# Seven block products for eight in the last two pairs of units, gate, value and output projection

## The chip, the cores and the metric

One core of one Trainium2 chip runs the program. The metric is device time in microseconds for one execution; the time before is the median of three runs.

## The reference

Chunk-selecting causal attention, then a gated feed-forward layer. For q, k, v of shape 4 x 8 heads x 768 x 64, keys stand in 24 chunks of 32; each query keeps the six chunks with the largest upper bound of its scores.

```python
ub = sum_d max(q * k_min[chunk], q * k_max[chunk])      # causal chunks only
top_chunks = argsort(ub)[..., -6:]
scores = where(selected & causal, q @ k.T / 8, -1e9)
x = softmax(scores) @ v                                  # laid out as 3072 tokens x 512
out = (sigmoid(x @ w_gate) * (x @ w_val)) @ w_out        # w_gate, w_val: 512 x 1536; w_out: 1536 x 512
```

The output is 3072 x 512 in float32.

## The kernel before

The 3072 tokens are taken in eight units u0 to u7 of 384 (three row tiles of 128). A unit first chooses chunks (`prepare`), then attends (`attend`: score products `sc`, exponentials `exp` on ACT, the causal mask `cm` on POOL, value products `pv`, and `finish`, which normalises on DVE with `rz` and `x` and turns x by a DMA transpose `xT` on SP for units u4 to u7), and then goes through the feed-forward layer. x of a unit lies as `xT`, four tiles of 128 channels by 384 tokens, in fp16; the three weight matrices stay in SBUF in fp16 (`wg16`, `wv16`, `wo16`).

Plain units (`ffn`, lines 898 to 927) make, for each of 12 blocks of 128 hidden columns, four gate matmuls and four value matmuls of 384 columns (line 913), `tanh` on ACT (line 921) and `hg = (tanh + 1) * value` on DVE (line 925), whose value operand is the product itself in PSUM. `project_out` (lines 929 to 957) then makes, for each of three row tiles, 12 matmuls of 512 columns (line 944; three instructions o0, o1, o2 of four), evicts on ACT or DVE with a factor 0.5 (`osb`, lines 953 and 954) and stores 256 KB through SP (`out`).

One pair of units, u5 with u6, goes through `ffn_pair` (line 977). Two units side by side, two halves of the channels and two halves of the hidden columns make 2 x 2 blocks, and seven products of blocks stand for eight. Four sums T of x blocks (line 993, DVE) and four sums each of gate and value weights (Sg, Sv in `mixed`, line 972, DVE) are formed first. For each of six pairs of hidden blocks, gate and value each need products P1 to P7 of two matmuls of 384 columns (line 1022), which collect in three PSUM banks. Three of the four results pass through SBUF: E (an eviction by ACT or DVE) and C (a sum on DVE, line 1037); the fourth stays in PSUM. `tanh` (line 1047) and `hg` (line 1052) follow, and for three of the four results `hg` reads its value from SBUF. Output projection of the pair is `project_out`, as for the others.

Nothing is ordered at run time. A string ORDER lists every instruction group in one sequence, with the engine where there is a choice (`@POOL`) and the numbers of the buffers it takes; each engine runs its share of the list in that order, and waits come from the data and from the reuse of buffers. There are eight PSUM banks (products named u, q, r, o, g, v share them), seven `np` buffers for the C sums, 18 `hg` buffers, six `v`, two `big`, two `qf` and one `qm`.

Of the kernel before, what the change touches and what calls it, by code (L numbers as in the profile page):

```python
# [162 lines left out]
sc_u3_7_2:2 v_3_1:5 rz_u3_1:0 x_u3_1:1 tanh_u2_7 sc_u3_4_0:5 exp_u3_4_0 cm_u3_4 hg_u2_7 exp_u3_7_2 exp_u3_4_2 hg_u2_6
sc_u3_7_1:0 exp_u3_7_1 g_u2_8:3,0,12 tanh_u2_8 v_u2_8:5 g_u2_9:7,1,13 sc_u3_4_1:3 v_u2_9:0 v_2_0:1 pv_u3_5:2
hq0_u4_0@POOL ubn0_u4:0 ubn1_u4 ubm0_u4 mx0_u4:0 ubm1_u4 hk0_2_3@DVE out_u1_2 tanh_u2_9 mx1_u4 hk0_2_2@DVE v_2_4:3
ap0_u4 apt0_u4:0 hk0_2_0@ACT hg_u2_8 g_u2_10:7,3,14 exp_u3_4_1 tanh_u2_10 v_u2_10:6 hg_u2_10 hg_u2_9 xps_u3_1:3,1
cm_u3_7 hq1_u4_2@POOL pv_u3_7:7 hq1_u4_0@POOL g_u2_11:1,2,15 v_u2_11:5 v_2_5:2 tanh_u2_11 hg_u2_11 o0_u2_0:6,1 o1_u2_0
xT_u3_1 hqm0_u4_0 sc_u4_1_3:3,0 exp_u4_1_3 hqm0_u4_2@DVE xps_u3_0:5 k11_3 qf0_u6_0:1 xT_u3_0 sc_u4_0_0:0,1 exp_u4_0_0
sc_u4_0_3:1 qf0_u5_1 qm_u5_0@ACT:0 pv_u3_4 rz_u3_2:0 x_u3_2:2 pv_u3_6 rz_u3_3:1 ap1_u4 x_u3_3:1 sc_u4_1_1:5 qf0_u6_3
k10_3 k16_3_3@DVE:6 sc_u4_1_2:0 exp_u4_1_2 qf0_u6_2 qf0_u5_2 qf0_u6_1 o2_u2_0 sc_u4_3_3:2,2 exp_u4_3_3 exp_u4_1_1  # L170
sc_u4_2_3:3,3 exp_u4_2_3 v_3_4:4 o0_u2_1:4,0 qm_u5_2 sc_u4_1_0:2 exp_u4_1_0 apt1_u4 sc_u4_0_2:5 exp_u4_0_2 o1_u2_1
v_1_5:0 sc_u4_2_1:2 exp_u4_2_1 kx0_3_1 kx1_3_3:1 kx0_3_0 hq1_u5_0@POOL sc_u4_2_0:5 v16_2_0 v16_2_4 v16_1_5 o2_u2_1
cm_u4_1 osb_u2_1 out_u2_1 sc_u4_0_1:2 exp_u4_0_1 exp_u4_0_3 k16_3_0:0 exp_u4_2_0 q10_3:1 osb_u2_0 out_u2_0 q00_3
sc_u4_3_1:3 exp_u4_3_1 ub_u5:7,0 ubn0_u5:0 hqm1_u4_0 pv_u4_1:5 sc_u4_5_0:6,0 cm_u4_0 pv_u4_0 rz_u4_0:1 sc_u4_4_0:3,1
xps_u3_2:7 xps_u3_3:1 hq0_u5_0@ACT o0_u2_2:2,0 sc_u4_5_1:4 o1_u2_2 hq1_u5_2@POOL exp_u4_5_0 exp_u4_4_0 xT_u3_3
hqm1_u4_2@DVE x_u4_0:1 o2_u2_2 xT_u3_2@ACT hk1_2_3@ACT exp_u4_5_1 g_u3_0:7,2,0 tanh_u3_0 sc_u4_5_2:4 exp_u4_5_2
sc_u4_5_3:5 sc_u4_4_3:3 exp_u4_4_3 v_u3_0:6 g_u3_1:7,1,12 tanh_u3_1 sc_u4_4_2:3 exp_u4_4_2 exp_u4_5_3 sc_u4_4_1:4
exp_u4_4_1 v_u3_1:1 g_u3_2:7,3,13 tanh_u3_2 ubn1_u5 v_u3_2:5 g_u3_3:4,0,14 hg_u3_0 tanh_u3_3 cm_u4_4 pv_u4_4:7 hk1_2_2
sc_u4_6_3:3,1 osb_u2_2 hq0_u5_2@POOL kx1_3_2 sc_u4_6_1:6 exp_u4_6_1 v_u3_3:0 sc_u4_3_0:2 exp_u4_3_0 v_3_0:0 v_2_3:3
v16_2_3 kx1_3_1 hg_u3_1 mx0_u5:0 hg_u3_2 sc_u4_6_0:4 cm_u4_5 pv_u4_5 g_u3_4:6,3,15 sc_u4_7_2:2,0 sc_u4_6_2:5 tanh_u3_4  # L180
cm_u4_2 exp_u4_6_2 hg_u3_3 exp_u4_6_3 v_u3_4:0 g_u3_5:6,0,2 tanh_u3_5 sc_u4_2_2:3 ap0_u5 sc_u4_7_0:5 exp_u4_7_0
exp_u4_6_0 cm_u4_6 v_u3_5:1 q01_3 g_u3_6:6,1,16 tanh_u3_6 v_u3_6:4 g_u3_7:6,2,17 tanh_u3_7 v_u3_7:5 apt0_u5:0
hqm0_u5_0 mx1_u5 q11_3 qf1_u6_1 qf1_u6_3 hg_u3_4 qf1_u6_2 ap1_u5 hg_u3_5 rz_u4_2:1 x_u4_2:2 xT_u4_2:0 hg_u3_6
qf0_u7_0:0 v_3_2:3 g_u3_8:4,1,1 tanh_u3_8 apt1_u5 qf1_u6_0 v16_2_5 v_u3_8:6 g_u3_9:7,0,3 sc_u4_3_2:4 tanh_u3_9 hg_u3_7
exp_u4_3_2 kx0_3_3 sc_u4_7_1:5 exp_u4_7_1 exp_u4_2_2 v_u3_9:1 exp_u4_7_2 sc_u4_7_3:7 exp_u4_7_3 hqm1_u5_2@DVE hg_u3_8
hqm0_u5_2@DVE g_u3_10:6,1,4 tanh_u3_10 cm_u4_3 pv_u4_6:5 v_3_3:1 pv_u4_3:3 hg_u3_9 sc_u5_0_2:1,1 exp_u5_0_2
sc_u5_0_0:2 sc_u5_1_1:7,2 sc_u5_0_1:6 exp_u5_0_1 exp_u5_0_0 pv_u4_2 rz_u4_1:1 x_u4_1:2 v_u3_10:1 hg_u3_10
qm_u6_2@ACT:0 hq1_u6_2@POOL cm_u4_7 pv_u4_7 hq0_u6_2 kx0_3_2 v_2_2:2 out_u2_2 g_u3_11:3,0,5 tanh_u3_11 sc_u5_3_0:1,0
sc_u5_7_1:2,3 v_u3_11:6 exp_u5_1_1 k16_3_1@ACT:5 v16_3_1 sc_u5_1_0:3 exp_u5_1_0 hq0_u6_0@POOL exp_u5_3_0 sc_u5_7_0:7
# [85 lines left out]
def pe(busy, lag=170):  # L275
    return {PE: (busy, busy + lag)}
# [3 lines left out]
def kernel(  # L280
# [10 lines left out]
    nc = tc.nc  # L291
# [667 lines left out]
    def mixed(w16, name, key, prio, raw):  # L959
# [10 lines left out]
        for i, x, op, y, need in ((0, a21, ALU.add, a22, []), (1, s(0), ALU.subtract, a11, [(t, 0)]),  # L970
# [3 lines left out]
            op.deps += [(o, False) for o in users]  # L974
        return t

    def ffn_pair(ua, ub_, base, span):

        next_ = rank(base, span, 6 * 32 + 2 * 15)
        EV = 0.1  # L980
# [225 lines left out]
```

## Time and profile before

| | |
|---|---|
| median of three runs | 290.27 us (290.11 to 291.36) |
| the profiled execution's own time | 289.61 us |
| its span in the profile | 287.9 us |
| busy: PE, DVE, ACT, POOL | 271.2, 222.2, 192.5, 115.3 us |
| granted TensorE clock | 1.00 |

The profile is of one execution. Busy time of an engine is the time in which at least one of its instructions ran; matmuls overlap one another, so the duration of one is longer than what it adds to the stream. The profiled execution's own time is larger than its span, since it holds what lies around the instructions, and it is one run beside the three of the median.

### The profile page before, as it was taken

Reading aid. Unit: us, or ns where it says so; the run is one execution under the profiler, and the core shown is the slowest. Engines: PE = TensorE matmul, PEld = TensorE weight load, DVE = VectorE, ACT = ScalarE, POOL = GpSimd, SP = SyncE. Lnnn points to the kernel's source line nnn. Section 1 sums busy time; section 2 is a strip of 40 time slices with the busy share of each in tenths; the row PEclk is TensorE's granted clock in tenths of the full one; section 3 lists DMA queues with packets and bytes.
Section 4 is the critical chain, followed back from the end, with each engine's and each line's share of the span. In section 5 each row is a group of like instructions: output and inputs, shape, how many; then the busy total and the mean of one; then the engine's idle time right before and its main releaser. Section 6 shows DMA issues by size and latency. Waiting matters only on the chain.

```text
span 287.9 us, 6927 instructions
## 1 busy us (share of the span) xinstructions
PE 271.2 (94%) x2596; PEld 173.0 (60%) x2596; DVE 222.2 (77%) x607; ACT 192.5 (67%) x403; POOL 115.3 (40%) x181
## 2 busy tenths in 40 slices
PE   1858999899999999999999999999999999999995
PEld 0636565667765666666767556578656666555543
DVE  7568987589998999996796999796899988831121
ACT  2477489697788876678759656578879996432320
POOL 7297735246166835656234874462131002000000
PEclk9999999999999999999999999999999999999999
DMA  7999999999999947969906221002300000101112
GB/s 162 242 231 221 214 196 201 211 176 218 184 192 193 207 88 134 215 130 184 182 20 149 59 68 50 2 14 67 88 28 2 15 16 12 56 36 73 53 59 109
DMA packets 130033, 34.26 MB, mean 119 GB/s; under 512 B 118096, under 2 KB 127056, under 8 KB 130000
## 3 DMA queue, kind: packets, MB, share of 16 engines
q1 hardware_dynamic: 125248, 29.11, 47.7%
q0 software_dynamic: 4752, 4.72, 9.8%
q8 instruction: 20, 0.33, 0.5%
q14 instruction: 13, 0.11, 0.1%
HBM read 30.67 MB, written 6.29 MB: 128 GB/s over the span
## 4 chain that ended last, share of the span: by engine, by line
PE 64%; DVE 13%; DMA 11%; ACT 4%; SPq 3%; issue 3%; POOL 1%; DVEq 0%; POOLq 0%; ACTq 0%
PE o_u L944 16%; PE v_u L913 11%; PE g_u L913 10%; PE sc_u L824 9%; PE pv_u L857 5%; DMA kq_u<-in_q_dram 4%; DMA v<-in_v_dram 3%; PE sug_u5u L1022 3%; PE suv_u5u L1022 3%; ACT att_u L835 2%; DVE hg_u L925 2%; SPq L503 2%; DMA q<-in_q_dram 2%; PE ube_u L763 2%; PE srv_u5u L1022 1%
## 5 line engine op out<-in xcount | busy, mean ns | idle before, releaser
L835 ACT ACTIVATE att_u<-sc_u 128x512 f16<-128x512 f32 (+3 forms) x184 | 90.8, 548 | 20.6 <-PE sc_u L824 19.4
L841 POOL TENSOR_SCALAR_AFFINE_SELECT att_u<-att_u 128x384 f16<-128x384 f16 (+1 forms) x56 | 30.0, 546 | 81.6 <-ACT att_u L835 71.4
L944 PE MATMUL o_u<-wo,hg_u 128*128 128x512 f16 (+1 forms) x252 | 59.5, 376 | 0.0
L913 PE MATMUL v_u<-xT_u,wv 128*128 128x384 f16 x288 | 58.6, 326 | 0.2 <-ACT gate_u L921 0.2
L913 PE MATMUL g_u<-xT_u,wg 128*128 128x384 f16 x288 | 58.6, 326 | 0.0
L925 DVE SCALAR_TENSOR_TENSOR hg_u<-gate_u,v_u 128x384 f16<-128x384 f16 x72 | 38.1, 541 | 25.0 <-PE v_u L913 16.3
L921 ACT ACTIVATE gate_u<-g_u 128x384 f16<-128x384 f32 x72 | 35.0, 494 | 24.0 <-PE g_u L913 23.5
L944 PEld LDWEIGHTS <-hg_u 128*128 128x128 f16 x264 | 24.5, 98 | 23.6 <-issue 0.7
L913 PEld LDWEIGHTS <-wv 128*128 128x128 f16 x288 | 27.5, 98 | 17.1 <-issue 1.4
L913 PEld LDWEIGHTS <-wg 128*128 128x128 f16 x288 | 27.2, 98 | 16.7 <-issue 0.5
L824 PE MATMUL sc_u<-hqo,hko 128*128 128x128 f16 (+2 forms) x220 | 27.9, 243 | 0.4 <-DVE osb_u L954 0.4
L857 PEld LDWEIGHTS <-att_u 128*128 128x128 f16 x640 | 24.6, 97 | 5.8 <-issue 1.9
L824 PE MATMUL sc_u<-hqe,hke 128*128 128x128 f16 (+2 forms) x220 | 27.8, 243 | 0.2 <-ACT att_u L835 0.2
L857 PE MATMUL pv_u<-v,att_u 128*128 128x65 f16 x640 | 26.9, 193 | 0.8 <-POOL v L540 0.7
L953 ACT ACTIVATE osb_u<-o_u 128x512 f32<-128x512 f32 (+1 forms) x17 | 10.1, 592 | 18.2 <-PE o_u L944 13.6
L824 PEld LDWEIGHTS <-hke 128*128 128x128 f16 x220 | 17.2, 98 | 7.5 <-issue 0.4
L824 PEld LDWEIGHTS <-hko 128*128 128x128 f16 x220 | 16.8, 98 | 6.0 <-issue 0.7
L540 POOL CAST v<-v 128x512 f16<-128x512 f32 x23 | 14.2, 620 | 9.4 <-DMA v<-in_v_dram 6.9
L876 DVE TENSOR_TENSOR x_u<-pv_u,rz_u 128x384 f16<-128x384 f32 (+1 forms) x28 | 14.8, 531 | 0.5
L786 DVE MAX8 mx_u<-ubn_u 128x8 f32<-128x8 f32 (+16 forms) x152 | 12.5, 156 | 0.1
L730 DVE STREAM_TRANSPOSE qf_u<-q 128x384 f32<-128x384 f32 (+2 forms) x28 | 11.8, 440 | 0.4 <-DMA q<-in_q_dram 0.3
L548 DVE TRANSPOSE_TENSOR_REDUCE kx<-k 128x24 f32<-128x768 f32 x12 | 11.2, 952 | 0.2 <-DMA k<-in_k_dram 0.2
(179 smaller groups left out, 450.5 us busy)
## 6 DMA issues: line engine op xcount, KB each, us to landing
v<-in_v_dram SPq DMA_DIRECT2D x23, 256.0 KB, 5.0
out_dram<-osb_u SPq DMA_DIRECT2D x23, 256.0 KB, 2.3
k<-in_k_dram SPq DMA_DIRECT2D x12, 384.0 KB, 5.5
q<-in_q_dram SPq DMA_DIRECT2D x12, 384.0 KB, 5.5
wg<-in_moe_w_gate_dram POOLq DMA_DIRECT2D x3, 512.0 KB, 10.3
wv<-in_moe_w_val_dram POOLq DMA_DIRECT2D x3, 512.0 KB, 11.5
wo<-in_moe_w_out_dram POOLq DMA_DIRECT2D x3, 512.0 KB, 19.0
qf<-in_q_dram SPq DMA_DIRECT2D x8, 128.0 KB, 3.3
```

The lines of the kernel that those rows point to most:

```text
L540: plan.add(f"v16_{b}_{ib}", {POOL: pool(H * D)}, lambda e: nc.gpsimd.tensor_copy(v16[b % 2][:, ib, :, 0:D], at(t)), reads=[t], writes=[("v ...
L786: nc.vector.max(at(mx)[:, e_, j, :], at(ubn)[:, e_, j, 0:max(8, u.seen[j])])
L824: nc.tensor.matmul(at(t)[:, o:o + 128 * m], hk[b % 2][e_][:, p, 128 * jb:128 * jb + 128], hq[u.side][e_][:, p, 128 * x:128 * (x + m)], sta ...
L835: plan.add(f"exp_{u.name}_{h}_{y}", {ACT: act(n)}, lambda e, t=t, att=att, b0=b0, n=n: nc.scalar.activation(at(att)[:, b0:b0 + n], at(t), ...
L841: nc.gpsimd.affine_select(out=dv, in_=dv, compare_op=ALU.is_ge, fill=0.0, base=0, pattern=[[0, u.m], [1, 128]], channel_multiplier=-1)
L857: nc.tensor.matmul(at(pv)[:, last, x, :], at(att)[:, c:c + 128], v16[b % 2][:, jb, h, :], start=(jb == 0), stop=(jb == ib))
L876: plan.add(f"x_{u.name}_{p}", {DVE: dve(u.t)}, lambda e: nc.vector.tensor_tensor(at(x_).rearrange("p a (e d) -> p e a d", e=2), at(pv)[:, ...
L913: nc.tensor.matmul(at(t), w16[:, c, 128 * fb:128 * fb + 128], at(u.xt)[:, c, :], start=(c == 0), stop=(c == 3))
L921: plan.add(f"tanh_{u.name}_{fb}", {ACT: act(T)}, lambda e, g=g, gate=gate: nc.scalar.activation(at(gate), at(g), AF.Tanh, scale=0.5), read ...
L925: plan.add(f"hg_{u.name}_{fb}", {DVE: dve(T)}, lambda e, w_=w_, gate=gate, hg=hg: nc.vector.scalar_tensor_tensor(at(hg), at(gate), 1.0, at ...
L944: nc.tensor.matmul(at(o), hgs[c][1][1]()[:, 128 * tb:128 * tb + 128], wo16[:, fc, lo:hi], start=(c == 0), stop=(c == NFB - 1))
L1022: nc.tensor.matmul(at(t), left[i](c), right[i](c), start=first and c == 0, stop=c == 1, skip_group_check=not first)
```

## The change

- Pairs are now u4 with u5 and u6 with u7; u6 is no longer paired with u5, and no unit after u3 goes through `ffn` or `project_out`.
- `ffn_pair` gets two parameters: where T lies (`qm` for the first pair, `qf` for the second) and whether the pair is the last one, whose `hg` of the second unit lies in `att` buffers. x of u6 and u7 share one buffer of eight tiles (`x0` is a unit's first tile in it).
- The output projection of a pair is also made of seven block products, in `project_pair`. Blocks are the two units, the two halves of the hidden columns and the two halves of the 512 output columns. For each of six pairs of hidden blocks four sums S1 to S4 of `hg` tiles (128 x 384, fp16, all operands in SBUF) are formed on DVE or POOL; S3 overwrites one of its inputs, the others go to buffers that attention has left (`v16`, `hq`, `hk`). Four sums So of w_out blocks are formed once on DVE (`mixed_out`).
- For each of three row tiles of a pair, products Q1 to Q7 of six matmuls of 256 columns collect in three PSUM banks. Each of the four output quarters starts with F (ACT or DVE, factor 0.5; one is F alone) and is completed by G (DVE, PSUM times 0.5 plus the quarter in SBUF). Q6, Q7 and Q4 add to a bank that F or G has read in between. The last tile of u7 is stored in two halves of 256 columns, all others as 512.
- ORDER is new from the point where u2's attention has ended and u3's has begun, ahead of u2's feed-forward layer, with other choices of engine for copies and evictions. Up to there it is the same.

```diff
+    def mixed_out():
...
+        b11, b12, b21, b22 = (wo16[:, a:a + half, n:n + 256] for a in (0, half) for n in (0, 256))
...
+        for i, x, y in ((0, b12, b11), (1, b22, t[0]), (2, b22, b12), (3, b21, t[1])):
+            op = plan.add(f"So{i}", {DVE: dve(D_FF, 1.8)}, lambda e, i=i, x=x, y=y: nc.vector.tensor_tensor(t[i], x, y, ALU.subtract),
...
+    def project_pair(ua, ub_, hg, homes, next_):
...
+        for f in range(half):
...
+            a11, a12, a21, a22 = hg[0, f], hg[0, f + half], hg[1, f], hg[1, f + half]
+            sums[3, f] = a21
+            for i, x, op_, y in ((1, a21, ALU.add, a22), (2, sums[1, f], ALU.subtract, a11), (3, a11, ALU.subtract, a21), (4, a12, ALU.subtract, sums[2, f])):
+                o = sums[i, f]
+                op = plan.add(f"S{i}_{tag}_{f}", {DVE: dve(T, 2), POOL: (960, 1000)}, lambda e, o=o, x=x, op_=op_, y=y: (
+                    nc.vector if e == DVE else nc.gpsimd).tensor_tensor(o[1](), x[1](), y[1](), op_),
...
+        what = {1: (11, lambda f: wo16[:, f, 0:256]), 2: (12, lambda f: wo16[:, f + half, 0:256]), 3: (4, lambda f: wo16[:, f + half, 256:512]),
+                4: (22, lambda f: so[3][:, f]), 5: (1, lambda f: so[0][:, f]), 6: (2, lambda f: so[1][:, f]), 7: (3, lambda f: so[2][:, f])}
...
+        for tb in range(3):
+            u_, q_, r_ = (ps(f"{c}o_{tag}_{tb}", c, [128, 256]) for c in ("su", "sq", "sr"))
...
+                    for f in range(half):
+                        nc.tensor.matmul(at(t), sums[what[i][0], f][1]()[:, 128 * tb:128 * tb + 128], what[i][1](f),
+                                         start=first and f == 0, stop=f == half - 1, skip_group_check=not first)
...
+            op = mul(1, u_, True)
...
+            keep_(0, u_, ka, oa, 0)
+            mul(2, q_, True)
+            add(0, q_, ka, oa, 0)
+            mul(5, r_, True)
+            keep_(3, r_, kb, ob, 256)
+            mul(6, u_, False)
+            keep_(1, u_, ka, oa, 256)
+            mul(3, r_, False)
+            add(1, r_, ka, oa, 256)
+            store(0, ka, oa, 0, 512)
+            mul(7, u_, False)
+            add(3, u_, kb, ob, 256)
+            mul(4, u_, False)
+            keep_(2, u_, kb, ob, 0)
+            if ub_ is units[7] and tb == 2:
+                store(1, kb, ob, 256, 512)
+                store(1, kb, ob, 0, 256)
+            else:
+                store(1, kb, ob, 0, 512)
...
-    ffn(units[4], 5.0, 0.95)
...
-    ffn_pair(units[5], units[6], 6.4, 1.6)
+    so = mixed_out()
+    ffn_pair(units[4], units[5], 6.0, 1.9, "qm", False)
...
-    ffn(units[7], 8.0, 0.95)
+    ffn_pair(units[6], units[7], 8.0, 1.9, "qf", True)
```

In ORDER, `mul`, `keep_` and `add` of `project_pair` are the entries Q, F and G.

More of the change, by code (lines that the diff above doesn't have):

```diff
@@ L163 @@
[L163 to L177, printed above, removed]
@@ L975, in mixed, with ffn_pair @@
         return t
-    def ffn_pair(ua, ub_, base, span):
+    def ffn_pair(ua, ub_, base, span, home, last):
         next_ = rank(base, span, 6 * 32 + 2 * 15)
@@ L996, in ffn_pair @@
         hgb = [Buf("v", f"hgp_{ub_.name}_{f}", [128, 2, T], F16) for f in range(half)]
+        if last:
+            hgb = [Buf("att", f"hgp_{ub_.name}_{f}", [128, 2, 2, T], F16) for f in range(0, half, 2) for _ in range(2)]
+            hgb = [hgb[f // 2 * 2] for f in range(half)]
         hg = {}
@@ L1078, in ffn_pair @@
                 plan.hold(first_, b)
-        for x, u in ((0, ua), (1, ub_)):
-            project_out(u, [(fb, hg[x, fb]) for f in range(half) for fb in (f, f + half)], [], next_)
+        if last:
+            out_home = Buf("big", f"osb_{tag}", [128, 3, 2, 512])
+            homes = {(tb, x): ((out_home, tb, x), lambda tb=tb, x=x: at(out_home)[:, tb, x]) for tb in range(3) for x in range(2)}
+        else:
+            home_ = Buf("qm", f"osb_{tag}", [128, 2, 512])
+            homes = {(1, x): ((home_, x), lambda x=x: at(home_)[:, x]) for x in range(2)}
+            for tb in (0, 2):
+                for x, u in ((0, ua), (1, ub_)):
+                    b = Buf("osb", f"osb_{u.name}_{tb}", [128, 512])
+                    homes[tb, x] = ((b, 0), lambda b=b: at(b))
@@ new lines, in ffn_pair, with held @@
+        project_pair(ua, ub_, hg, homes, next_)
+    def held(keys):
+        found = {}
+        for key in keys:
+            if key in plan.writer:
+                found[plan.writer[key]] = False
+            for o in plan.readers.get(key, ()):
+                found[o] = False
+        return list(found.items())
+    def mixed_out():
+        views = [hk[0][e].rearrange("p a s -> p (a s)").rearrange("p (i f n) -> p i f n", i=2, n=256) for e in range(2)]
+        half = NFB // 2
+        b11, b12, b21, b22 = (wo16[:, a:a + half, n:n + 256] for a in (0, half) for n in (0, 256))
+        t = [views[i // 2][:, i % 2] for i in range(4)]
+        free = held([("hk", 0, jb, e, p) for jb in range(NBLK) for e in range(2) for p in range(NP)] +
+                    [("hkp", 0, e, p) for e in range(2) for p in range(NP)])
+        for i, x, y in ((0, b12, b11), (1, b22, t[0]), (2, b22, b12), (3, b21, t[1])):
+            op = plan.add(f"So{i}", {DVE: dve(D_FF, 1.8)}, lambda e, i=i, x=x, y=y: nc.vector.tensor_tensor(t[i], x, y, ALU.subtract),
+                          reads=[("wo", j) for j in range(3)] + ([("So", i // 2)] if i % 2 else []), writes=[("So", i)], port=True, prio=6.9 + 0.02 * i)
+            op.deps += [d for d in free if d not in op.deps]
+        return t
@@ L1082 @@
     for u in units:
-        u.xt = Buf("qf" if u.i >= 7 else "xt", f"xT_{u.name}", [128, 4, T], F16)
+        u.xt, u.x0 = Buf("xt", f"xT_{u.name}", [128, 4, T], F16), 0
+    units[6].xt = units[7].xt = Buf("qf", "xT_u6u7", [128, 8, T], F16)
+    units[7].x0 = 4
     raw_f = {b: load_first(b, -10.0 + b) for b in range(3)}
```

284 lines of the change are left out of this document (189 added, 95 removed).

## Prediction

> **What bounds the kernel now.** I read the page's engine shares first, then the waits of PE after its start-up, then busy time by windows, and last the chain of waits with the tables by form, for what one instruction costs.
>
> ```profile
> PE 271.2 (94%) x2596; PEld 173.0 (60%) x2596; DVE 222.2 (77%) x607; ACT 192.5 (67%) x403; POOL 115.3 (40%) x181
> ```
>
> ```profile
> PE ube_u L763 <- DVE hg_u L925: 0.4, 1, 0.4
> PE sc_u L824 <- DVE osb_u L954: 0.4, 1, 0.4
> PE v_u L913 <- ACT gate_u L921: 0.2, 1, 0.2
> ```
>
> ```profile
> 0.00:20.00 20.00, 9.98 (x67) 7.54 (x67) 11.85 (x23) 8.42 (x13) 12.31 (x26) 1.00 0.94 210
> 20.00:40.00 20.00, 18.73 (x155) 12.62 (x156) 18.64 (x72) 12.98 (x29) 12.97 (x20) 1.00 1.20 214
> 40.00:60.00 20.00, 18.97 (x191) 12.00 (x190) 12.83 (x44) 16.54 (x44) 8.77 (x19) 1.00 1.03 194
> ...
> 212.00:252.00 40.00, 40.00 (x360) 25.62 (x358) 36.75 (x78) 31.83 (x72) 2.98 (x6) 1.00 0.07 18
> ...
> 280.00:288.00 8.00, 4.67 (x34) 2.65 (x32) 0.98 (x2) 0.63 (x2) 0.00 (x0) 1.00 0.26 98
> ```
>
> The three waits are all that PE has from 60 us to the end: 1.0 us in sum. The windows' columns are PE, weight load, DVE, ACT and POOL busy, then the granted clock, the DMA share and GB/s. Of 16.7 us in which PE is idle (287.9 less 271.2), 12.3 lie before 60 us, in start-up, and 3.3 behind the last matmul. In between, PE is the bound: a microsecond of matmul taken out there shortens the run by one, unless another engine takes the place. DVE is the next candidate: in the stage where the one existing block-product pair runs (212 to 252 us) it is busy 36.75 of 40 us with 78 instructions, yet PE waited for nothing. POOL worked only 2.98 us there. That row is the yardstick below.
>
> **PE: what goes and what comes.**
>
> ```profile
> 231.43 0.65 PE suv_u5u L1022 x4
> ...
> 241.30 0.91 PE pv_u L857 x30
> ...
> 248.49 0.65 PE g_u L913 x4
> ...
> 258.71 5.18 PE o_u L944 x24
> ```
>
> ```profile
> L944 PE MATMUL o_u<-wo,hg_u 128*128 128x512 f16 x240 | 57.6, 379 | 0.0
> ...
> L824 PE MATMUL sc_u<-hqo,hko 128*128 128x256 f16 x44 | 9.4, 273 | 0.0
> ```
>
> In the chain, four matmuls of 384 columns take 0.65 us (0.1625 each, plain or block product alike), and 24 of 512 take 5.18 (0.216 each). The durations by form include a latency that overlaps the next matmul: 379 ns for 512 columns against 216 of advance. With 256 columns fewer the duration is 106 ns shorter (273), so such a matmul advances PE by about 0.109 us. Weight loads keep up: the page has 173.0 us for 2596 of them, 67 ns each. Gone: the plain gate and value of units u4 and u7, 2 x 96 matmuls x 0.1625 = 31.2 us; the plain projection of u4 to u7, 4 x 36 x 0.216 = 31.1 us (one tile is split in two, same columns). New: one more gate/value pair, 6 x 2 x 7 products x 2 matmuls = 168 x 0.1625 = 27.3 us; two projections, 2 x 3 row tiles x 7 products x 6 matmuls = 252 x 0.109 = 27.5 us. Net **-7.5 us**. The other pair exists already and only changes partners. These are upper values of what the products save; nothing else leaves PE.
>
> **DVE, ACT, POOL: what the products cost elsewhere.** The second pair adds 36 evictions E (ACT or DVE), 36 sums C (DVE) and four T. The projections add 48 sums S (35 on POOL, 13 on DVE), four So and, for six evictions of 512 columns per pair, 12 F and 9 G of 256. The new order moves copies off DVE: 58 instead of 73. I weigh this where it must fit tightest: the last stage, from T0 of u6/u7 to its first projection product Q1.
>
> ```profile
> 222.21 0.54 DVE L1037 TENSOR_TENSOR c3g_u5u<-c3g_u5u,sug_u5u 128x384 f32<-128x384 f32 x1
> 222.67 0.54 DVE L1037 TENSOR_TENSOR c1g_u5u<-c1g_u5u,srg_u5u 128x384 f32<-128x384 f32 x1
> ```
>
> ```profile
> L635 DVE TENSOR_TENSOR xf<-pvf,rzf 128x256 f16<-128x256 f32 x8 | 3.3, 418 | 0.1
> ...
> L972 DVE TENSOR_TENSOR Sg<-wg 128x1536 f16<-128x1536 f16 x2 | 1.8, 912 | 0.0
> ...
> L555 POOL TENSOR_TENSOR kcr<-kx,kcr 128x96 f32<-128x96 f32 x2 | 0.8, 388 | 0.1
> ...
> L555 POOL TENSOR_TENSOR kcr<-kx_u,kcr 128x48 f32<-128x48 f32 x1 | 0.3, 276 | 0.0
> ```
>
> Sums start 0.46 us apart though each shows 0.54; so DVE's own advance is 0.08 below the duration. The written order puts into that stage, on PE, 84 gate/value products x 0.325, 21 products of the u4/u5 projection x 0.655 and two attention products of 15 matmuls each (30 take 0.91 in the chain): 42.0 us. On DVE: 34 C and 24 hg x 0.465 = 27.0; 11 G and F of 256 columns x 0.33 = 3.6; two So x 0.87 = 1.7; four T x 0.46 = 1.8; seven S, taken as 0.27 (half a T of twice the width; at most 0.46) = 1.9; two for the last normalisation, at most 0.9. Together 84 instructions, 36.9 us. That is 2.0 per us of PE, where the yardstick has 1.95 and PE does not wait. ACT has no exponentials left there and is under 30 us. So by load alone PE keeps its lead, with about 5 us of room.
>
> What the yardstick lacks is POOL. Two points of POOL's tensor-tensor (276 ns at 48 columns, 388 at 96) give 2.33 ns a column, so an S of 384 takes about 1.06 us, an estimate along that line; 21 of them and one mask are 23 us in the 42, against 2.98 in 40 now.
>
> ```profile
> 208.63 1.31 POOL L841 TENSOR_SCALAR_AFFINE_SELECT att_u<-att_u 128x384 f16<-128x384 f16 x2 [5.65 <-ACT att_u L835]
> 210.00 1.03 POOL L333 COPY hqo<-apt_u 64x768 f16<-64x768 f16 x1
> ```
>
> ```profile
> 206.22 0.55 DVE L993 TENSOR_TENSOR T_u5u<-xT_u,xT_u 128x768 f16<-128x768 f16 x1
> ...
> 210.27 1.17 DVE L993 TENSOR_TENSOR T_u5u<-xT_u 128x768 f16<-128x768 f16 x1
> ```
>
> ```profile
> L1052 DVE SCALAR_TENSOR_TENSOR hgp_u<-gate_u5u,c1v_u5u x6: 551/552/679, 220.7 to 250.4; 128x384 f16<-128x384 f16 x6
> ```
>
> A T takes 0.55 us with POOL idle, and 1.17 when begun inside POOL's copy (210.00 to 211.03): it ends about 0.4 us after that copy, as if it had stood still until then. One hg, whose gate and sum both lie in SBUF, took 679 ns instead of 552. The page "SBUF — State Buffer" of the Trainium skill, section "Who interferes with whom", says that a DVE instruction with two SBUF inputs and a GpSimd instruction that reads SBUF exclude each other for a whole instruction, the later one waiting; this trace agrees for the T (1.17 against 0.55), and the rule speaks against putting S on POOL beside hg.
>
> In the last stage 31 DVE instructions read two SBUF tensors: 18 of the 24 hg (the other six take PSUM), seven S, two So, four T. C, G and F read PSUM. If POOL is inside an instruction for 23 of 42 us and a collision costs half an S (0.53 us), 31 x 0.55 x 0.53 = 9 us would be added to DVE's 36.9, 3.9 more than PE's 42.0. Bounds: no collisions, zero; every one of the 31 meeting a running S, 16.4 us added, 11.3 over. I take **+2.5 us**, nearer the middle estimate than zero, since POOL's S come in bursts and a queued S must then wait for DVE in turn. In the u4/u5 pair before it, attention of u6 and u7 lies between, so PE has more to do per DVE instruction; I put stalls there at zero. If that cover fails, the price is again some 0.5 us per collision.
>
> **The end, and the queues.**
>
> ```profile
> out_dram<-osb_u SPq DMA_DIRECT2D x23, 256.0 KB, 2.3
> ```
>
> The row 280 to 288 has PE busy for its first 4.67 us: its last matmul ends at 284.67, and eviction and last store take the 3.2 us to 287.9. After the change the last eviction has 256 columns and its store half of this row's 256 KB: no loss, and a gain that I leave at zero. But six row tiles of u6 and u7 leave together: 1.5 MB in about the last 5 us, where the row 280 to 288 shows 98 GB/s at a DMA share of 0.26, that is 377 GB/s at full use or 4.2 us for them. They nearly fit; I add **0.3 us** (0 to 0.7). On SP the stores queue only behind one another. What may stall at the seam is T1 and T3 of u6/u7, which wait for the transpose by DMA of u7's last head pair and hold the DVE instructions ordered behind them (G, F and S of u4/u5). Ahead of the first product that needs them PE has nine projection products and two gate products, 6.5 us, against about 1 for normalising and a transfer like the stores' 2.3: hidden, and if not, some 1 us.
>
> Two dependencies are new on PE: the weights' differences So stand on DVE well ahead of the products that read them, so nothing; and products 6, 7 and 4 add into the bank that F and G have just read, so each waits for that read. In the order two or three products (1.3 to 2.0 us) of other row tiles lie between, once only one (0.65 us), for a read of about 0.4: zero, at most 0.3.
>
> **The sum.** Against the profiled execution: span 287.9 - 7.5 + 2.5 + 0.3 = 283.2 us; its own time is 289.61, 1.7 above its span, and the median of the runs, 290.27, lies 0.66 higher still. Carried over, 290.27 - 4.7 = **285.6 us**.
>
> **Rivals.**
> - No contention that counts: POOL's S fall beside C, G and F, which do not meet it. For: six of ten DVE instructions in the stage are of that kind, and POOL has 19 us to wait in. Against: the 1.17 us row. 290.27 - 7.5 + 0.3 = 283.1 us. Chance 0.22.
> - DVE and POOL become the bound of the last stage, slower than before. Place: from T0 of u6/u7 to Q1; price per collision 0.53 us. It decides from the point where the waits exceed the 5.1 us of room by the 7.2 that are left of the gain: 12.3 us, 0.40 us on each of the 31. With every one of them meeting an S: 290.27 - 7.5 + 0.3 + 11.3 = 294.4 us. For: all S of a unit pair wait for the hg that run at the same time. Against: POOL has work for only 55% of the stage. By the Trainium skill's rule (same page and section), taken strictly, the middle estimate of 3.9 would stand instead of 2.5, and the sum would be 287.0. Chance 0.16.
> - The new order leaves holes of its own, for instance at the seam or in the redrawn middle part, where half of the 7.5 us vanish from PE while DVE gets more to do. One hole as long as the seam's whole cover, 6.5 us, eats the gain: 290.27 - 7.5 + 0.3 + 6.5 = 289.6 us. Chance 0.10.
> - That the change does not do what it says is excluded by the listing of instructions: 588 pair and projection matmuls of u4 to u7 stand where 516 of larger size stood.
>
> **How the numbers follow.** The forecast, 284 to 288 us, has 0.52. A measurement of this kernel can tell about 0.5% (1.5 us) from no change. Faster by more than that (below 288.8): forecast 0.52, no contention 0.22 and a tenth of the third rival, 0.75. Within it: 0.09, the rest of the third rival. Slower: 0.16. The range goes from 282.0 (no contention, and the whole 1.0 us of PE's present waits gone) to 291.5, which takes in the third rival and the weak end of the second.
>
> **What would show it.** In the profile after: PE with about 36 matmuls of 512 columns for each of u0 to u3 only, and 252 of 256 columns at an advance of 0.11; PE busy about 264 us. POOL's S near 1.06 us each. In the last 55 us, hg with both inputs in SBUF at a mean clearly above 552 ns, C unchanged at 550, and PE's waits of 2 to 4 us naming hg, E or S. Wrong it would be if PE waits before that stage, if hg keeps 552 ns beside a busy POOL, or if PE's waits name POOL's S alone.

## The result and the profile after

| | before | after |
|---|---|---|
| median of four runs each, side by side | 290.19 us | 285.88 us |
| ratio, 95% interval | | 0.986 [0.982, 0.990] |
| the profiled execution, span | 287.9 us | 284.5 us |
| busy PE, DVE, ACT, POOL | 271.2, 222.2, 192.5, 115.3 us | 265.6, 248.8, 209.5, 162.1 us |

The forecast was 285.6 us. A second comparison, of six runs with 17 of before, gave 0.988 [0.983, 0.993].

The page's engine shares of after, and then the waits of PE from 60 us to the end (engine, tile and line, what it waited for; us in total, times, longest):

```profile
PE 265.6 (93%) x2668; PEld 180.9 (64%) x2668; DVE 248.8 (87%) x660; ACT 209.5 (74%) x457; POOL 162.1 (57%) x231
```

```profile
PE sqg_u4u L1054 <- DVE x_u L900: 0.7, 1, 0.7
PE srg_u6u L1054 <- DVE hg_u L1084: 0.5, 1, 0.5
PE sug_u4u L1054 <- DVE c3g_u4u L1069: 0.3, 1, 0.3
...
```

All rows of that view together hold 1.9 us, against 1.0 before. Busy time by windows of after (PE, weight load, DVE, ACT, POOL, granted clock, DMA share, GB/s):

```profile
200.00:220.00 20.00, 19.14 (x186) 12.53 (x185) 19.46 (x39) 18.63 (x43) 13.57 (x17) 1.00 0.08 17
220.00:240.00 20.00, 19.48 (x198) 15.01 (x196) 18.56 (x42) 12.22 (x31) 6.00 (x7) 1.00 0.19 63
240.00:260.00 20.00, 19.72 (x133) 12.82 (x132) 19.16 (x39) 14.19 (x36) 7.35 (x8) 1.00 0.04 14
260.00:280.00 20.00, 19.89 (x161) 15.52 (x159) 16.54 (x35) 9.62 (x24) 10.25 (x11) 1.00 0.13 50
223.07:266.54 43.47, 42.63 (x323) 29.43 (x322) 41.09 (x85) 28.93 (x72) 15.96 (x17) 1.00 0.14 48
280.00:285.00 5.00, 0.96 (x9) 0.59 (x7) 0.10 (x1) 0.77 (x2) 0.00 (x0) 0.84 0.61 229
```

Where before had PE busy for 40.00 of 40 us beside DVE's 36.75, DVE is now busy for 41.09 of the 43.47 us of the row 223.07 to 266.54, which is the last stage. PE is idle in each of these windows, a little in each. The last row has PE busy for its first 0.96 us, so the last matmul ends at 280.96, 3.5 us ahead of the span's end. Groups by form on DVE and POOL (count | busy us, mean ns of one | idle before):

```profile
L1084 DVE SCALAR_TENSOR_TENSOR hgp_u<-gate_u4u,c3v_u4u 128x384 f16<-128x384 f16 x6 | 4.8, 801 | 0.0
L1084 DVE SCALAR_TENSOR_TENSOR hgp_u<-gate_u4u,c1v_u4u 128x384 f16<-128x384 f16 x6 | 4.5, 748 | 0.0
L1084 DVE SCALAR_TENSOR_TENSOR hg_u<-gate_u6u,c0v_u6u 128x384 f16<-128x384 f16 x6 | 4.4, 735 | 0.1
L1084 DVE SCALAR_TENSOR_TENSOR hgp_u<-gate_u6u,c1v_u6u 128x384 f16<-128x384 f16 x6 | 4.1, 684 | 0.3
L1084 DVE SCALAR_TENSOR_TENSOR hg_u<-gate_u4u,c0v_u4u 128x384 f16<-128x384 f16 x6 | 4.1, 684 | 0.2
L1084 DVE SCALAR_TENSOR_TENSOR hgp_u<-gate_u6u,c3v_u6u 128x384 f16<-128x384 f16 x6 | 3.9, 645 | 0.4 <-ACT gate_u6u L1079 0.2
...
L1069 DVE TENSOR_TENSOR c0g_u6u<-c0g_u6u,sqg_u6u 128x384 f32<-128x384 f32 x6 | 3.3, 548 | 0.5 <-ACT c0g_u6u L353 0.5
...
L1084 DVE SCALAR_TENSOR_TENSOR hg_u<-gate_u6u,suv_u6u 128x384 f16<-128x384 f16 x6 | 3.2, 546 | 0.1
```

```profile
L1177 POOL TENSOR_TENSOR hgp_u<-hg_u,hgp_u 128x384 f16<-128x384 f16 x8 | 7.7, 965 | 0.1
```

The six groups of hg with two inputs in SBUF stand at 645 to 801 ns, 25.8 us for 36. The form whose value is in PSUM keeps 546, and C, which reads PSUM, keeps 548. POOL's 35 sums S add up to 34.9 us over all their forms, 1.0 us each.

How one late hg reaches PE can be read from the chain of waits (start us, us, what):

```profile
251.61 0.55 DVE c0g_u6u L1069
...
252.88 0.85 DVE hgp_u L1084
...
254.47 0.54 DVE c3g_u6u L1069
255.01 0.47 DVE c1g_u6u L1069
255.47 0.68 DVE hg_u L1084
...
256.23 0.49 ACT c1v_u6u L353
...
256.76 0.48 PE suv_u6u L1054 x2
```

Two hg of 0.85 and 0.68 us stand on DVE among the sums C. After them ACT evicts, and then PE gets its next product. From 251.5 to 256.8 us the chain that set the end runs over DVE and ACT, with a single product of 0.50 us on PE in between.

**A finer measure than the whole run.** The part ahead of the pairs differs from execution to execution: the first product of the pair u4/u5 starts between 176.39 and 179.36 us over the profiled executions of the nine kernels below that share the order up to it. From there on the two profiled executions of after agree within 0.1 us. So I also compare stretches between marks on PE: the first product of u4/u5, the first projection product of u4/u5 and the first of u6/u7. PE's timeline in after, a first reading:

```profile
176.48 0.48 PE L1054 MATMUL srg_u4u<-T_u4u,Sg 128*128 128x384 f16 x2 [0.22 <-DVE T_u4u L1019]
...
223.07 0.81 PE L1195 MATMUL suo_u4u<-wo,hg_u 128*128 128x256 f16 x6
...
266.38 0.82 PE L1195 MATMUL suo_u6u<-wo,hg_u 128*128 128x256 f16 x6
```

The stage of u4/u5 takes 46.59 us, the last stage 43.31, and from the first mark to the end of the span it is 108.0. A second profiled execution of after gave 46.59, 43.30 and 108.0.

### The profile page after: what moved, and what is told of

Read it like the earlier page. It is cut to its first block, busy times and chain, and to the rows that moved or that the text cites. A ratio compares the mean times of both kernels' runs of the same rounds, so it can differ in the third digit from the quotient of the medians.

```text
span 284.5 us, 7266 instructions
## 1 busy us (share of the span) xinstructions
PE 265.6 (93%) x2668; PEld 180.9 (64%) x2668; DVE 248.8 (87%) x660; ACT 209.5 (74%) x457; POOL 162.1 (57%) x231
## 4 chain that ended last, share of the span: by engine, by line
PE 66%; DVE 11%; DMA 9%; SPq 4%; ACT 3%; POOL 3%; issue 2%; DVEq 0%; POOLq 0%; ACTq 0%
PE sc_u L848 9%; PE o_u L968 9%; PE g_u L937 8%; PE v_u L937 8%; PE pv_u L881 5%; DMA kq_u<-in_k_dram 5%; DMA v<-in_v_dram 4%; PE suo_u6u L1195 3%; PE suo_u4u L1195 2%; PE ube_u L787 2%; PE suv_u6u L1054 2%; DVE hg_u L1084 2%; PE sug_u6u L1054 2%; DVE hgp_u L1084 2%; SPq L538 2%
## 5 line engine op out<-in xcount | busy, mean ns | idle before, releaser
L937 PE MATMUL g_u<-xT_u,wg 128*128 128x384 f16 x192 | 39.1, 326 | 0.1
L937 PE MATMUL v_u<-xT_u,wv 128*128 128x384 f16 x192 | 39.0, 326 | 0.1
L968 PE MATMUL o_u<-wo,hg_u 128*128 128x512 f16 x144 | 35.3, 379 | 1.0 <-DMA wo<-in_moe_w_out_dram 1.0
L949 DVE SCALAR_TENSOR_TENSOR hg_u<-gate_u,v_u 128x384 f16<-128x384 f16 x48 | 25.1, 535 | 4.3 <-PE v_u L937 2.4
L881 PE MATMUL pv_u<-v,att_u 128*128 128x65 f16 x640 | 27.3, 193 | 1.1 <-POOL v L564 1.0
L945 ACT ACTIVATE gate_u<-g_u 128x384 f16<-128x384 f32 x48 | 23.3, 495 | 6.7 <-PE g_u L937 6.5
L848 PE MATMUL sc_u<-hqo,hko 128*128 128x128 f16 (+2 forms) x220 | 27.3, 243 | 0.1
L937 PEld LDWEIGHTS <-wg 128*128 128x128 f16 x192 | 18.1, 98 | 10.4 <-issue 0.8
L937 PEld LDWEIGHTS <-wv 128*128 128x128 f16 x192 | 18.1, 98 | 10.5 <-DMA wv<-in_moe_w_val_dram 0.4
L968 PEld LDWEIGHTS <-hg_u 128*128 128x128 f16 x144 | 13.2, 98 | 13.7 <-DVE kcr L572 1.3
L1054 PEld LDWEIGHTS <-Sg 128*128 128x128 f16 x96 | 9.1, 98 | 6.1 <-issue 1.4
L1054 PEld LDWEIGHTS <-Sv 128*128 128x128 f16 x96 | 9.0, 98 | 5.4 <-issue 0.5
```

The source lines that it names most:

```text
L848: nc.tensor.matmul(at(t)[:, o:o + 128 * m], hk[b % 2][e_][:, p, 128 * jb:128 * jb + 128], hq[u.side][e_][:, p, 128 * x:128 * (x + m)], sta ...
L881: nc.tensor.matmul(at(pv)[:, last, x, :], at(att)[:, c:c + 128], v16[b % 2][:, jb, h, :], start=(jb == 0), stop=(jb == ib))
L937: nc.tensor.matmul(at(t), w16[:, c, 128 * fb:128 * fb + 128], at(u.xt)[:, c, :], start=(c == 0), stop=(c == 3))
L945: plan.add(f"tanh_{u.name}_{fb}", {ACT: act(T)}, lambda e, g=g, gate=gate: nc.scalar.activation(at(gate), at(g), AF.Tanh, scale=0.5), read ...
L949: plan.add(f"hg_{u.name}_{fb}", {DVE: dve(T)}, lambda e, w_=w_, gate=gate, hg=hg: nc.vector.scalar_tensor_tensor(at(hg), at(gate), 1.0, at ...
L968: nc.tensor.matmul(at(o), hgs[c][1][1]()[:, 128 * tb:128 * tb + 128], wo16[:, fc, lo:hi], start=(c == 0), stop=(c == NFB - 1))
```

## The experiments

Theory A: POOL's sums, reading SBUF, hold up the hg beside them, and PE stalls for it. Theory B: DVE is simply too full. Theory C: the written order has holes, whatever POOL does. Times are medians; each job had 17 runs of before, with medians of 290.9, 290.84 and 291.1 us.

| kernel | us | ratio, 95% interval | stage u4/u5 | last stage | first mark to end |
|---|---|---|---|---|---|
| after, again | 287.39 | 0.988 [0.983, 0.993] | 46.59 | 43.30 | 108.0 |
| no sums S | 283.6 | 0.9745 [0.970, 0.979] | 44.95 | 41.33 | 104.6 |
| sums formed, read by nobody | 288.66 | 0.990 [0.985, 0.994] | 46.57 | 43.49 | 108.0 |
| fills in place of POOL's sums | 283.91 | 0.974 [0.970, 0.978] | 44.97 | 41.34 | 104.4 |
| all sums on DVE | 294.84 | 1.013 [1.008, 1.019] | 48.20 | 47.87 | 114.8 |
| nine more sums on DVE | 290.73 | 0.998 [0.995, 1.001] | 46.59 | 45.25 | 110.8 |
| plain projection, both pairs | 289.57 | 0.997 [0.993, 1.001] | | | 110.0 |
| plain projection, u6/u7 | 287.78 | 0.989 [0.986, 0.991] | 46.59 | | 108.1 |
| plain projection, u4/u5 | 290.37 | 0.998 [0.996, 1.001] | | | 109.8 |

**The changed kernel again**, as the yardstick of the first job.

> The changed kernel once more, timed beside the three that follow. All theories: near 285.9 us, a ratio near 0.985 to the kernel before.

It came out at 0.988, and the rest of its row above shows how well a profile repeats once the part ahead of the pairs is left out.

**No sums S.** All S are left out of the order, and the products read the unsummed tiles, so that the output is no longer that of the reference:

```diff
-            sums[3, f] = a21
-            for i, x, op_, y in ((1, a21, ALU.add, a22), ...):
-                ...S on DVE or POOL
+            sums[1, f], sums[2, f], sums[3, f], sums[4, f] = a21, a22, a21, a12
```

> Leaves out the 48 sums S1 to S4 of the output projections; the products Q read hg tiles unsummed in their place, with the same matmuls. A (S on POOL and DVE's instructions with two SBUF inputs block each other, and that makes PE wait): hg with both inputs in SBUF falls from a mean of 716 ns to 552 to 580, PE's lost time of the u4/u5 stage and the last stage (about 3 us) goes nearly whole, 283.0 us (282.4 to 283.8). B (DVE is simply too full there): DVE loses only 13 short S, about 4 us of its 249, so some 0.5 us, 285.4. C (the holes belong to the written order, whatever S does): 285.9.

283.6 us, as A said. PE is busy for 20.00 us in each stretch of 20 from 200 to 260, and the last stage takes 41.33 us, which is what its matmuls need (82 gate/value products x 0.325, 21 of projection x 0.655 and 0.91 for attention make 41.3). But this takes away the sums' wait for hg, the products' wait for the sums and 13 sums of DVE as well. Two later runs separate these.

**Sums formed, but read by nobody; then fills in their place.** The first keeps every S at its place and lets the products read other tiles. The second makes of each S on POOL three fills of the same buffer. In both the output is no longer that of the reference.

```diff
-                o = sums[i, f]
+                o = sums[i, f] if i != 3 else sums[1, f]
...
+        for f in range(half):
+            sums[1, f], sums[2, f], sums[3, f], sums[4, f] = hg[1, f], hg[1, f + half], hg[1, f], hg[0, f + half]
```

```diff
-                    nc.vector if e == DVE else nc.gpsimd).tensor_tensor(o[1](), x[1](), y[1](), op_),
+                    nc.vector.tensor_tensor(o[1](), x[1](), y[1](), op_) if e == DVE else
+                    [nc.gpsimd.memset(o[1](), 0.0) for _ in range(3)]),
```

> The changed kernel with all 48 sums S still formed at their places (35 on POOL, 13 on DVE), but read by nobody on PE: the products Q take unsummed hg tiles, and S3 writes over S1's buffer instead of over hg. So the output is not that of the reference. Left are POOL's reads beside hg; gone is every wait of a product for a sum. A (POOL's S hold up the hg that read two SBUF tensors): no gain, ratio to before 0.985 to 0.991 (286.5 to 288.2 us), as the changed kernel's 0.988; hg of that form 645 to 800 ns. Rival (what cost time was that products waited for sums, not the reads): like the kernel without S, 0.9745 (283.4 us).

> As the kernel whose S are read by nobody, but each of the 35 sums on POOL is three fills of the same buffer (128x384, fp16) at the same place, which wait for the same hg and read no memory. So the output is not that of the reference. POOL stays about as busy, the masks stay queued behind as much work. A: hg goes back to about 550 ns, ratio to before 0.973 to 0.979 (283.0 to 284.8 us). Rival (masks and buffers are held up by POOL's queue, whatever it does): 0.985 to 0.991, as the changed kernel, with hg at 550 ns.

Both ratios came out as A said. With the sums read by nobody the time stays (0.990). With fills it falls to 0.974, though POOL is busier than in after. Groups by form, first of the kernel with unread sums, then of the one with fills, and the latter's timeline of PE:

```profile
L1084 DVE SCALAR_TENSOR_TENSOR hgp_u<-gate_u4u,c3v_u4u 128x384 f16<-128x384 f16 x6 | 4.8, 799 | 0.0
L1084 DVE SCALAR_TENSOR_TENSOR hg_u<-gate_u6u,c0v_u6u 128x384 f16<-128x384 f16 x6 | 4.5, 748 | 0.1
```

```profile
PE 263.4 (94%) x2668; PEld 180.5 (64%) x2668; DVE 242.6 (86%) x660; ACT 209.2 (74%) x457; POOL 169.4 (60%) x301
...
L1178 POOL MEMSET v<- 128x384 f16 x60 | 24.5, 418 | 6.5 <-DVE v L1177 3.0 <-PE pv_u L881 1.1
...
```

```profile
L1084 DVE SCALAR_TENSOR_TENSOR hg_u<-gate_u4u,c0v_u4u 128x384 f16<-128x384 f16 x6 | 4.1, 687 | 0.2
L1084 DVE SCALAR_TENSOR_TENSOR hgp_u<-gate_u4u,c3v_u4u 128x384 f16<-128x384 f16 x6 | 3.5, 576 | 0.0
L1084 DVE SCALAR_TENSOR_TENSOR hg_u<-gate_u6u,c0v_u6u 128x384 f16<-128x384 f16 x6 | 3.3, 552 | 0.1
```

```profile
177.12 0.48 PE L1054 MATMUL srg_u4u<-T_u4u,Sg 128*128 128x384 f16 x2 [0.21 <-DVE T_u4u L1019]
...
222.09 0.82 PE L1198 MATMUL suo_u4u<-wo,hg_u 128*128 128x256 f16 x6
...
263.43 0.82 PE L1198 MATMUL suo_u6u<-wo,hg_u 128*128 128x256 f16 x6
```

hg is back at 550 to 576 ns, but for one form at 687. That form stands at 690 in the kernel without any sum, too: two of its six took 1168 and 760 ns there, and both began while POOL ran a cast of a tile in SBUF; the other four took 549 to 559. So it is the same collision with another reader on POOL, which all these kernels have. The last hg of one form and what POOL runs beside it, in after and then with fills:

```profile
225.47 0.90 POOL L1177 TENSOR_TENSOR hgp_u<-hg_u,hgp_u 128x384 f16<-128x384 f16 x1
...
225.81 0.98 DVE L1084 SCALAR_TENSOR_TENSOR hgp_u<-gate_u4u,c3v_u4u 128x384 f16<-128x384 f16 x1
```

```profile
224.31 1.37 POOL L1178 MEMSET hqo<- 128x384 f16 x3
...
224.57 0.55 DVE L1084 SCALAR_TENSOR_TENSOR hgp_u<-gate_u4u,c3v_u4u 128x384 f16<-128x384 f16 x1
```

Taken one by one in after, the order of starting decides. Of the 36 hg with two inputs in SBUF, the 18 that began while POOL ran an instruction that reads SBUF took 565 to 1273 ns; the other 18 took 544 to 558, also those in which a sum on POOL began. Of the 35 sums on POOL, the 12 that began inside a DVE instruction with two inputs in SBUF took 1027 to 1227 ns, the other 23 took 902 to 921.

The u4/u5 stage is 1.6 us shorter than in after and the last stage 2.0. So the 3.6 us are lost to what POOL's sums read, not to POOL being busy, nor to its queue, nor to products that wait for sums. The Trainium skill, "SBUF — State Buffer", section "Who interferes with whom", says that a DVE instruction with two SBUF inputs contends with a GpSimd instruction that reads SBUF and not with one that only writes it; these two runs agree (hg 799 ns beside sums, 576 beside fills).

**All sums on DVE, and nine more of them.** Only the engine is changed, at the same places in the order; in the second, every second of the 18 sums of u6/u7 on POOL.

```diff
-... S2_u6u7_1@POOL ... S1_u6u7_0@POOL S2_u6u7_0@POOL S3_u6u7_0@POOL ...
+... S2_u6u7_1@POOL ... S1_u6u7_0 S2_u6u7_0@POOL S3_u6u7_0 ...
```

> All 48 S on DVE, at the same places of the order; POOL makes none. A: hg with both inputs in SBUF back to 552 to 580 ns, 36 x 0.16 = 6 us less for hg on DVE, against 35 x 0.27 = 9.5 us more for S: nearly even, 285.4 to 286.9. B: DVE gets fuller by the whole 9.5 us in stages where it has about 5 us of room: 288 to 290. C: 285.9.

> The changed kernel with every second of the 18 POOL sums of the last pair on DVE, same places in the order; the computation is unchanged. A: nine sums fewer beside hg, half of the last stage's 2.2 us of stalls gone, but 9 x 0.35 = 3.2 us more on DVE, which had 5 us of room: 0.984 to 0.988 (286.2 to 287.4 us), no worse than the changed kernel. B (DVE is full, a sum queued ahead of C and hg delays PE by what it takes): 9 x 0.35 = 3.2 us later less the 1.1: 0.993 to 0.997 (289 to 290 us).

A's numbers fell in both. The second lies a little above B's, and the first far above them: 294.84 us against 288 to 290. hg was free of collisions with sums in the first, 548 to 575 ns but for the one form at 687, and yet it is slower than before. The waits of PE in it, and then in the second:

```profile
PE suo_u4u L1193 <- DVE hqo L1175: 1.5, 1, 1.5
PE suv_u6u L1052 <- DVE c0v_u6u L1067: 1.4, 1, 1.4
```

```profile
PE suv_u6u L1053 <- DVE c1v_u6u L1068: 1.0, 1, 1.0
...
PE suo_u6u L1194 <- DVE hg_u L1083: 0.6, 1, 0.6
```

DVE runs its list in order, so a sum queued ahead of a C or an hg delays the bank or the tile for which PE waits, and a sum in the queue can itself be late for its product (the first row, 1.5 us). By the marks, and beside the kernel with fills, 35 sums on DVE cost 114.8 - 104.4 = 10.4 us, 0.30 each; the same 35 on POOL cost 108.0 - 104.4 = 3.6 us, 0.10 each. The move itself costs the difference: 0.19 us for each of the 35, and 0.31 for each of the nine (2.8 us). On DVE a sum costs PE nearly the 0.35 us that it takes there: there is hardly room for it, which is B. B is not what made after lose its 3.6 us, and its figure for the move of all 35 was too low; but moved to DVE, the sums cost more by B than they did by A on POOL.

**POOL's reads by themselves.** The kernel before, with 24 instructions added on POOL in the stage of the pair u5/u6. In one they add two weight tiles in SBUF into a spare buffer, in the other they only fill it.

```diff
+        plan.add(f"D{n}", {POOL: (960, 1000)}, lambda e: nc.gpsimd.tensor_tensor(
+            decoy_out, wg16[:, 0, 0:T], wg16[:, 1, 0:T], ALU.add), reads=[("wg", 0)], writes=["decoy_out"])
```

```diff
+        plan.add(f"D{n}", {POOL: (960, 1000)}, lambda e: [nc.gpsimd.memset(decoy_out, 0.0) for _ in range(3)], writes=["decoy_out"])
```

> The kernel before with 24 idle sums on POOL spread over the stage of its one pair (tensor-tensor, 128 x 384 fp16, both inputs in SBUF, result read by nobody): POOL then works some 25 us in the 40 in which it now works 2.98. A: hg with both inputs in SBUF goes from 552 ns to 680 to 750, DVE's 36.75 of 40 us fill up, PE begins to wait: 1 to 3 us slower, 291.2 to 293.2. B and C: no change, 290.2, hg at 552 ns.

> The same with POOL only writing: 24 times three fills of 128 x 300 float32, again some 25 us of POOL in the stage, at the same places. A: a POOL instruction that reads no SBUF does not meet hg: hg at 552 ns, 290.2 us. A variant in which any busy POOL hinders DVE: like the run with reads, 291 to 293. B and C: 290.2.

294.5 us, 1.011 [1.008, 1.014], and 293.65 us, 1.009 [1.005, 1.012]. The reads cost time, as A has it, and more than its 291.2 to 293.2 us; but the fills, for which A had 290.2 us, cost almost as much. Groups by form with reads, then with fills, and the latter's longest wait of PE:

```profile
L1053 DVE SCALAR_TENSOR_TENSOR hg_u<-gate_u5u,c0v_u5u 128x384 f16<-128x384 f16 x6 | 5.1, 846 | 0.1
```

```profile
L1053 DVE SCALAR_TENSOR_TENSOR hg_u<-gate_u5u,c0v_u5u 128x384 f16<-128x384 f16 x6 | 3.6, 607 | 0.1
...
PE pv_u L858 <- POOL att_u L842: 1.7, 2, 0.9
```

As to hg, A is right: this form has 846 ns beside reads, 607 beside fills. What I had left out is that the causal masks stand on POOL behind the added instructions, and the value product waits for them. PE's timeline gives the price of each: from the pair's first product to the 24 projection matmuls behind it, in the kernel before, with reads, and with fills:

```profile
207.66 0.49 PE L1022 MATMUL srv_u5u<-T_u5u,Sv 128*128 128x384 f16 x2
...
258.55 5.34 PE L944 MATMUL o_u<-wo,hg_u 128*128 128x512 f16 x24
```

```profile
210.39 0.49 PE L1023 MATMUL srv_u5u<-T_u5u,Sv 128*128 128x384 f16 x2
...
264.94 5.34 PE L945 MATMUL o_u<-wo,hg_u 128*128 128x512 f16 x24
```

```profile
208.91 0.49 PE L1023 MATMUL srv_u5u<-T_u5u,Sv 128*128 128x384 f16 x2
...
262.01 5.34 PE L945 MATMUL o_u<-wo,hg_u 128*128 128x512 f16 x24
```

50.89, 54.55 and 53.10 us: the fills lose 2.2 us and the reads 3.7, which is 1.5 more. How much of the reads' 3.7 us the masks account for is not shown: waits for them stand at 1.7 us with fills and at 0.6 with reads. Alone, this pair of runs would have been a weak test. The fills at the sums' own places, above, are the clean one, since there the masks' queue is as long either way.

**Plain projection.** Gate and value stay block products; the output projection of both pairs, of u6/u7 alone or of u4/u5 alone is plain again, with the order of its entries drawn by hand.

```diff
+        if True:        # or: if last / if not last
+            for x, u in ((0, ua), (1, ub_)):
+                project_out(u, [(fb, hg[x, fb]) for f in range(half) for fb in (f, f + half)], [], next_)
+            return
```

> Pairs u4/u5 and u6/u7 keep gate and value as block products, but project out plainly as before (matmuls of 512 columns, no S, So, F and G): PE gets 3.6 us more (31.1 for 27.5). A: the stalls of about 3 us go with S, 286.0 to 287.0, so the block products of the projection would be worth next to nothing. B: DVE loses G and 13 S, a third of the stalls goes, 288.5. C: 289.5.

> Only the last pair u6/u7 projects out plainly (its 24 S, its F and G and seven of eight products for it go; So and the u4/u5 projection stay): PE gets 1.8 us more. A: the last stage keeps only the S of u4/u5 at its head, about 1.5 us of stalls go: 285.9 to 286.7. B and C: 287.3 to 287.7.

> Only the first pair u4/u5 projects out plainly: PE gets 1.8 us more, 24 S fall away, 12 of them beside the u4/u5 gate and value products and the others at the seam. A: about 1 us of stalls goes: 286.3 to 287.2. B and C: 287.3 to 287.7.

For u6/u7 it is the same as after: 0.989 against 0.988, and 108.1 us behind the first mark against 108.0. In that pair the block-product projection saves PE 1.8 us (half of 31.1 - 27.5), and its sums take about as much back. In us, 287.78 lies nearer to B's and C's figures than to A's; but all of these were reckoned from after at 285.9, and after itself came at 287.39 when it was run again. I go by the distance to after, by the marks: 0.1 us here, where A had 0 to 0.8, B and C 1.4 to 1.8. The other two are slower than after, and A is missed in both. With both plain the distance is 2.0 us, for A's 0.1 to 1.1, B's 2.6 and C's 3.6; with u4/u5 plain it is 1.8 us, which is what B and C had (1.4 to 1.8). Waits of PE with both projections plain:

```profile
PE srg_u6u L1044 <- ACT c3g_u6u L343: 0.7, 1, 0.7
PE suv_u6u L1044 <- DVE c0v_u6u L1059: 0.7, 2, 0.4
```

The same two stand in the run with u4/u5 plain, and neither engine is full there (DVE 15.58 of the 20 us from 240 to 260 with both plain). With both plain PE is idle for 1.6 us between 220 and 280 us, where without sums it is idle for none up to 260. Without such holes, 104.4 + 3.6 = 108.0 us behind the first mark would be due with both plain, and 104.4 + 1.8 + 2.0 = 108.2 with u4/u5 plain. Measured are 110.0 and 109.8. I put the 1.6 to 2.0 us of difference down to my hand-drawn order, which is C, but of my own making; this is argued, as an order without these holes was not tried. So what the projection of u4/u5 brings by itself is only argued from the sum: 1.8 us saved, 1.6 lost.

No version tried beats the changed kernel with the whole computation in it.

## Why the prediction was right

It said 285.6 us, and 285.88 was measured. By its steps:

- **PE's matmuls, -7.5 us: right.** The forecast was about 264 us of PE busy. Without collisions it is 263.4 (fills) and 263.9 (no sums). In after it is 265.6 with the same 2668 matmuls. In the two stages PE is busy for 87.75 us (45.28 and 42.47), with fills for 85.93 (44.59 and 41.34): of the 3.6 us lost, 1.8 are counted as busy time of the same products, and so stand in no wait.
- **The mechanism: right.** hg with two inputs in SBUF at 716 ns on average, C unchanged, S on POOL at 1.0 us for an estimated 1.06. On DVE an S took 0.35 us for an assumed 0.27.
- **Its size in the last stage: +2.5 forecast, 2.0 measured, but by a working that fails.** I had POOL in an instruction for 23 of 42 us, 0.29 us for each of 31 instructions, 9 us on DVE. POOL was busy for 15.96 of the stage's 43.47 us, and the 18 hg there were longer by 0.14 us each (735, 684 and 645 ns against 552). DVE was busy for 2.9 us more in that stage than with fills (40.94 against 38.09), not for 9. And I compared sums of busy time: DVE's 36.9 us beside PE's 42.0 gave 5.1 us of room that collisions first had to fill. DVE is busy for 41.09 us, which is still less than 42.0, and PE stalls all the same. PE waits for single results, C and hg, that come late by one collision; room elsewhere in the stage does not give that back. I had too much time for collisions and counted on too much room; that the two nearly cancelled, and 2.5 came near 2.0, is luck.
- **No stall in the u4/u5 stage: wrong, 1.6 us.** This was the step that failed, and by the prediction's own sign (PE waits before the last stage) it was wrong here. I had cover from the attention of u6 and u7 there; DVE's busy time of 19.46 us in the 20 from 200 to 220 shows that it was at least as full as in the last stage. The stage is 46.59 us with sums and 44.97 with fills. Even with fills DVE is busy for 43.30 us of it, beside 44.59 of PE.
- **The end, +0.3: right.** 3.5 us behind the last matmul instead of 3.2.
- **The sum** with the measured terms is 287.9 - 7.5 + 1.6 + 2.0 + 0.3 = 284.3 us, for a span of 284.5; the forecast span was 283.2. The medians fell by 4.3 us, near the forecast 4.7, and the profiled spans by only 3.4: before's profiled execution lies 0.6 us below its median, after's 0.6 above. The interval of the ratio (2.9 to 5.2 us) holds both, so that the stalls, 1.1 us more than forecast, do not show in the time. In the second comparison the medians fell by 3.5 us. That the first came within 0.3 us of the forecast is luck, too.
- **The rivals.** No contention, 283.1 us: the runs without it gave 283.6 and 283.9, so the figure was good and its condition absent. DVE as the bound, 294.4 us: it did not happen with the sums on POOL, but moving the sums to DVE gave 294.84, by another way. Holes of the new order, 289.6 us: with fills PE is idle for 0.4 us in the u4/u5 stage and for none in the last, so there is no such hole. Taking the rule of the Trainium skill ("SBUF — State Buffer", section "Who interferes with whom") strictly would have given 287.0; its +3.9 us was nearer to the 3.6 lost in all, though all of it was put into the last stage.
- **What would show it** was right for hg, C and S, and wrong for the waits: PE's rows name hg in the last 55 us, but with 0.5 us, not 2 to 4, and the longest wait, 0.7 us, lies in the stage before.

By this sum the block-product projection, half of what is new, brought about nothing here (3.6 us off PE, 3.6 us lost to its sums), and the second pair's gate and value (31.2 - 27.3 = 3.9 us) make up most of the gain. A run shows it for u6/u7 alone; the kernel with both projections plain is 2.0 us slower than after, which I put down to its order.

## What to carry to other kernels

Before a helper instruction is moved to POOL, see whether it reads SBUF while DVE has instructions with two inputs in SBUF; price it by what PE loses per instruction on either engine (here 0.10 us on POOL, 0.30 on DVE), not by busy time left over. A sum of busy times does not tell whether PE stalls: with 38.1 us of DVE beside 41.3 of PE in the last stage, as the fills have it, collisions that added 2.9 us to DVE cost PE 2.0. Look for the instruction whose one result PE waits for next. And compare two kernels between marks on PE behind the part that varies: here that resolved 0.1 us where whole runs of one kernel differ by up to 3.

## What the runs showed of the hardware

Fills on POOL, 418 ns for 128x384 fp16, cost PE nothing at the sums' places with POOL busy for 18.27 of the 20 us from 220 to 240. I had not expected this to be so exact beside a DVE that is busy for 92% of the last stage: it takes 41.34 us with fills and 41.33 with nothing. It does not hold at any place: in the kernel before, fills ahead of the masks cost 2.2 us. A sum of 128x384 fp16 took 0.91 us on POOL undisturbed, 1.03 to 1.23 when it began inside a DVE instruction with two inputs in SBUF, and 0.35 on DVE.
